# An attention and two-MoE kernel on one core: a third buffer for queries and keys, and another order of the first loads

## The chip, the cores and the metric

The kernel runs on one core of a Trainium2 chip. A core has TensorE (PE, matmuls; PEld is its weight load), VectorE (DVE), ScalarE (ACT) and GpSimd (POOL), an SP queue that issues the DMAs, on-chip memory (SBUF) and eight matmul result banks (PSUM). The metric is the device time in microseconds of one execution; lower is better. Before the change three runs gave 1020.78, 1024.65 and 1021.84 us, so the median is 1021.84 us.

## The reference

The input has 4 batches, 8 heads, 576 positions, head size 64. Cut to what matters:

```python
cum    = cumsum(maximum(s, 0), axis=-1)            # one row of running sums per head
scores = q @ k.T / sqrt(64) - (cum[:, None] - cum[None, :])   # the second part at most 0
attn   = softmax(where(causal, -1e9, scores))
x      = (attn @ v) as 2304 x 512
x      = ((x @ w_a) * (x @ w_b)) @ w_out           # 512 -> 1536 -> 512
out    = maximum(x @ w_in2, 0)**2 @ w_out2         # 512 -> 2048 -> 512
```

The weights of the MoE parts come as 64-bit floats; the kernel decodes their words on the chip.

## The kernel before

The work of all engines is recorded as operations, and a planner (`Plan.order`, a list scheduler with cost guesses per operation) fixes the order in which each engine issues them. Every engine then works its own list in order, so an instruction that waits holds all that stand behind it on its engine. The planner knows a rank per stream ("first" before "att", "moe", "late", "fill"), the buffers of each tag, and a `lag` by which an operation may be held back. Where it sees TensorE idle it puts filler matmuls (tile `glow`, weights and data `warm`) in the gap, which keep TensorE's clock up, and where a gap is longer than 400 ns it gives the next operation some more (`idle`).

Attention is done head by head. For batches 0 and 1 (`WHOLE = 2`) the query and the key of one head are loaded into the tiles `fq` and `fk` as 64 rows, a 65th row holds ones or the running sums, and one matmul in 32-bit floats (two records in the trace) gives a block of scores in a bank `st`. VectorE takes each block's maximum (`neg`), ScalarE the exponentials (`e`), TensorE transposes them (`pt`), either engine copies them (`ph`), TensorE multiplies with the values (`av`), and `u` is divided by the sums and stored to `xd`. For batches 2 and 3 two heads are loaded at a time (`raw`), scaled and split into high and low parts in tiles `T` (T1), `t2q`, `t2k`; each block is then two shorter matmuls. There the maximum is an instruction that also masks; the order calls it ISA, the profile CUSTOM_DVE.

The buffers that matter: two query tiles `fq` (tag T2q), used by head number modulo 2, and two `fk` (tag T2k); `t2q` and `t2k` of batches 2 and 3 take the same tags. The `raw` tiles have two buffers of their own, which the first sums also use (`ssb`, `spos`, `ch`, `cl`). So head 2 can load its query only when head 0's score blocks are done.

While the first batches' attention runs, the weights w_a, w_b and w_out are loaded (512 KB each, into room tiles `roomxh`, `roomxl`, `words`) and decoded on VectorE, ScalarE and GpSimd (`words`, `decode`). The first MoE matmuls (`ab`, `py`) start between attention work. Later chunks of x are read back from `xd` into `xl` and split (`xh`), and the words of w_in2 are decoded as well (`w2ir`, `w2it`). After about 400 us there is only matmul work with little else around it.

At the start the program issues fillers, and before the first score block of heads 0 and 2 it has six more:

```python
if b == 0 and i == 0 and hh in (0, 2):
    pl.ops[-1].idle = 6
```

Of the kernel before, what the change touches and what calls it, by code (L numbers as in the profile page):

```python
# [7 lines left out]
F32 = mybir.dt.float32  # L8
F32R = mybir.dt.float32r
# [254 lines left out]
def attention_moe_moe(tc, q, k, v, s, w_a, w_b, w_out, w_in2, w_out2, out):  # L264
# [61 lines left out]
    def at(shape, dtype, tag, bufs, name):  # L326
        return gated("at", shape, dtype, tag, bufs, name)
# [8 lines left out]
    def pe(cost, calls, out, ins, lag=0.0):  # L336
        pl.add({"PE": (cost, calls, False)}, [out], ins, lag=lag)
# [71 lines left out]
    kb = [(0, HEAD)] + [(HEAD + BODY * i, BODY) for i in range((S - HEAD) // BODY)]  # L409
    LAST = len(kb) - 1  # L410

    def load_values(b, p):

        t = at([P, NJ, P], F32, "val", 2, f"val{b}_{p}")
        j = 0
        while j < len(kb):
            k0, m = kb[j]
            j1 = j + 1
            while j1 < len(kb) and kb[j1][1] == m:
                j1 += 1  # L420
            dma(
                t[:m, j:j1].part(j),
                v[b, p, k0 : k0 + m * (j1 - j)].rearrange("(j t) c -> t j c", t=m), m * (j1 - j) * 0.5,
            )
            for i in range(j, j1):
                values[b, p, i] = t[:m, i].part(j)
            j = j1
# [2 lines left out]


    WHOLE = 2
    first_q = [at([P, S], F32, "T2q", 2, f"fq{i}") for i in range(2)]
    first_k = {}

    def load_first(b, hh):
        tq = first_q[hh % 2]
        tk = first_k[b, hh] = at([P, S], F32, "T2k", 2, f"fk{b}_{hh}")
        dma(tk[:D].part("x"), k[b, hh], S * 0.25)
        dma(tq[:D].part("x"), q[b, hh], S * 0.25)  # L440

# [3 lines left out]
    glow = mm_bank("glow")  # L445
    pl.stream = "fill"
    for i in range(FILL):
        pe(310, [("matmul", (glow, warm[:, :P], warm), {"start": True, "stop": True})], glow, [warm])
    pl.stream = "first"

    ssb = at([P, S], F32, "raw", 2, "ssb")[: B * H]
    dma(ssb, s.rearrange("b h s -> (b h) s"), 74)
    for hh in range(2):
        load_first(0, hh)

    ident = const([P, P], F32, "ident")
# [15 lines left out]
    plain = at_const([P, P], BF16, "plain")  # L472
    act("copy", P, plain, ident)

    spos = at([P, S], F32, "raw", 2, "spos")[: B * H]
    dve("tensor_scalar_max", S, spos, ssb, 0.0)
    cum = at([P, S], F32, "kh", 1, "cum")[: B * H]
    dve("tensor_tensor_scan", S, cum, spos, spos, 0.0, ALU.add, ALU.bypass)
    for t in first_q:
        gps("memset", S, t[D : D + 1].part("c"), 1.0)  # L480
    ch, cl = (at([P, S], F32R, "raw", 2, z)[: B * H] for z in ("ch", "cl"))
    act("copy", S, ch, cum)
    dve("tensor_tensor", S, out=cl, in0=cum, in1=ch.bitcast(F32), op=ALU.subtract, two=True)
    dma(cd[:, 0, :].part(0), ch.bitcast(F32), 74)
# [18 lines left out]
    RUNS = {(0, 1), (336, 0), (336, 2)}  # L503

    def load_pair(b, p, src, nm):
        t = at([P, S], F32, "raw", 2, f"raw{nm}")
        dma(t, src[b, 2 * p : 2 * p + 2].rearrange("h d s -> (h d) s"), 288)
        return t

# [23 lines left out]
    def prep_first(b, p):  # L533

        load_values(b, p)
        heads = []
        for hh in (2 * p, 2 * p + 1):
            if (b, hh) not in first_k:
                load_first(b, hh)
            tk = first_k[b, hh]  # L540
            dma(tk[D : D + 1].part("c"), cum[b * H + hh : b * H + hh + 1], 2)
            tq = first_q[hh % 2]
            scaled(S, tq[:D].part("x"))
            heads.append((tq, tk))
        return heads

    def prep(b, p):

        nm = f"{b}_{p}"
        tq = load_pair(b, p, q, f"{nm}q")  # L550
        tk = load_pair(b, p, k, f"{nm}k")
        load_values(b, p)
        scaled(S, tq)
        heads = []
        for h in range(2):
            hh = b * H + 2 * p + h
            t1 = operands()
            t2q = at([P, S], F32R, "T2q", 2, f"t2q{nm}_{h}")
            t2k = at([P, S], F32R, "T2k", 2, f"t2k{nm}_{h}")
            dma(t1[64:66, 1].bitcast(F32).part("ck"), cd[hh], 5)  # L560
            up, dn = slice(0, 64), slice(64, 128)
            xq, xk = t1[up, 0].part("xq"), t1[up, 1].part("xk")
            if h == 0:
                copy(S, xk, tk[up])
                copy(S, xq, tq[up])
                dma(t2q[up].bitcast(F32).part(0), xq.bitcast(F32), 144)
                subtract(S, t2q[dn].part(1), tq[up], xq.bitcast(F32))
                subtract(S, t2k[up].part(0), tk[up], xk.bitcast(F32))
                dma(t2k[dn].bitcast(F32).part(1), xk.bitcast(F32), 144)
            else:  # L570
                hi = t2q[dn].part(1)
                copy(S, hi, tq[dn])
                dma(xq.bitcast(F32), hi.bitcast(F32), 144)
                subtract(S, t2q[up].part(0), tq[dn], hi.bitcast(F32))
                hi = at([P, S], F32, "kh", 1, f"kh{nm}")[dn]
                copy(S, hi.bitcast(F32R), tk[dn])
                dma(xk.bitcast(F32), hi, 144)
                dma(t2k[up].bitcast(F32).part(0), hi, 144)
                subtract(S, t2k[dn].part(1), tk[dn], hi)
            heads.append((t1, t2q, t2k))  # L580
        return heads
# [4 lines left out]
    def softmax(b, p, h, head, one):  # L586
# [11 lines left out]
        for i, pieces in enumerate(banks):  # L598
            ps = mm_bank(f"st{nm}_{i}") if b == 0 and i % 4 > 1 else bank(f"st{nm}_{i}")
            off = 0  # L600
            calls, cost, got = [], 0, []
            for blk, k0, kn in pieces:
                at_, m = kb[blk]
                qc = slice(at_, at_ + m)
                to = ps[:m, off : off + kn]
                diag = at_ >= k0 and at_ + m <= k0 + kn
                ks = slice(k0, k0 + kn)
                if b < WHOLE:
                    tq, tk = head
                    both = ((tq[: D + 1, qc], tk[: D + 1, ks]),)  # L610
                    cost += 4 * kn / 2.4 + 13
                else:
                    t1, t2q, t2k = head
                    both = ((t1[:66, 0, qc], t1[:66, 1, ks]), (t2q[:, qc], t2k[:, ks]))
                    cost += 2 * (kn / 2.4 + 15)
                calls += [("matmul", (to, *ab), {"stop": True}) for ab in both]
                if diag and b < MASKED:
                    tri = mask[:m, EDGE : EDGE + m]
                    calls.append(("matmul", (to[:, kn - m :], plain[:m, :m], tri), {"stop": True}))
                    cost += 70  # L620
                e, eo = place[blk]
                got.append((blk, k0, m, to, kn, diag, e[:m, eo + k0 : eo + k0 + kn]))
                off += kn
            if b < WHOLE:
                ins = [tq.part("x"), tq.part("c"), tk.part("x"), tk.part("c")]
            else:
                ins = [t1, t2q, t2k]
            if b < MASKED:
                ins += [plain, mask]

            for z, (_, _, kw) in enumerate(calls):
                kw.update(start=z == 0, skip_group_check=z > 0)
            pe(cost, calls, ps, ins)
            if b == 0 and i == 0 and hh in (0, 2):
                pl.ops[-1].idle = 6
            for blk, k0, m, to, kn, diag, _ in got:
                c = blk if k0 == 0 else nq
                if not diag or b < MASKED:
                    dve("tensor_reduce", kn, out=neg[:m, c : c + 1].part(c), in_=to, op=ALU.max, axis=AX.X, negate=True)
                    continue  # L640
                edge = EDGE + m
                dve(
                    "tensor_tensor_reduce", kn + 135, out=to, in0=to, in1=mask[:m, edge - kn : edge], op0=ALU.add,
                    op1=ALU.min, scale=-1.0, scalar=3.0e38, accum_out=neg[:m, c : c + 1].part(c),
                )
            held += got
            whole = [x for x in held if x[0] != LAST or pieces[0][0] == LAST]
            held = [x for x in held if x not in whole]
            if pieces[0][0] == LAST:
                dve(  # L650
                    "tensor_reduce", 2, out=neg[:, nq + 1 : nq + 2].part(nq + 1), in_=neg[:, nq - 1 : nq + 1],
                    op=ALU.min, axis=AX.X, reads=[neg.part(nq - 1), neg.part(nq)],
                )
            for blk, k0, m, to, kn, diag, ee in whole:
                c = blk if k0 == 0 else nq
                n_ = nq + 1 if blk == LAST else blk
                act(
                    "activation", kn + 360, ee.part((blk, k0)), to, AF.Exp, bias=neg[:m, n_ : n_ + 1].part(n_), scale=-1.0 if diag and b >= MASKED else 1.0,
                    accum_out=tot[:m, blk, int(c == nq) : int(c == nq) + 1].part(c), psum=True,
                )  # L660
# [939 lines left out]
```

## Time and profile before

| | |
|---|---|
| median of three runs | 1021.84 us |
| profiled execution, its time | 1023.91 us |
| its span, first to last instruction | 1022.1 us |
| TensorE busy | 1002.8 us (98%) |
| VectorE, ScalarE, GpSimd busy | 735.5, 603.9, 322.3 us |
| DMA | 240.58 MB, mean 235 GB/s |

The trace shows when each instruction began, how long it took and what ended the idle time before it. A matmul's end is modelled, so a busy TensorE may still lose time between matmuls.

### The profile page before, as it was taken

To read this page: it belongs to the slowest core of one execution; us is meant where nothing else is said; L and a number is where in the kernel's file an instruction comes from. 1 tells how busy PE (TensorE), PEld (TensorE's weight loads), DVE (VectorE), ACT (ScalarE), POOL (GpSimd) and SP (SyncE) were. 2 spreads that over 40 slices of the span, in tenths; PEclk is the share of its full clock that TensorE was granted. 3 is DMA by queue.
4 is the path that set the end of the run, shared out by engine and by line. 5 is a ranking of instruction groups with operands and counts; after the bars stand their busy time and mean duration, and the time that the engine had idled before them with its cause. 6 is when DMAs were issued, how large, how long until landed. Compare 5 with 4: busy or idle time off the path is not lost.

```text
span 1022.1 us, 16764 instructions
## 1 busy us (share of the span) xinstructions
PE 1002.8 (98%) x5612; PEld 867.8 (85%) x5619; DVE 735.5 (72%) x1546; ACT 603.9 (59%) x1373; POOL 322.3 (32%) x293
## 2 busy tenths in 40 slices
PE   9999999999999999999999999999999999999997
PEld 5766777777777778788889999999999999999997
DVE  5878876756677765565697898688767755876566
ACT  6777886565777643343344544487565766657552
POOL 2243134325454622101122323323335212431123
PEclk9999999999999999999999999999999999999999
DMA  7458896558778667857666668499968876678664
GB/s 226 131 157 256 273 288 186 152 150 258 228 199 246 185 212 262 275 183 233 206 207 207 208 206 273 164 336 363 344 219 322 313 260 231 246 273 319 220 233 165
DMA packets 138006, 240.58 MB, mean 235 GB/s; under 512 B 21320, under 2 KB 91072, under 8 KB 137920
## 3 DMA queue, kind: packets, MB, share of 16 engines
q1 hardware_dynamic: 137920, 239.52, 71.1%
q8 instruction: 44, 0.72, 0.3%
q14 instruction: 42, 0.34, 0.1%
HBM read 181.42 MB, written 52.11 MB: 228 GB/s over the span
## 4 chain that ended last, share of the span: by engine, by line
PE 75%; DMA 5%; DVE 2%; SPq 1%; ACT 1%; issue 0%; DVEq 0%; ACTq 0%
PE ab L261 14%; PE pa L261 9%; PE py L261 8%; PE po_0t L261 6%; PE pw L261 5%; PE pc L261 5%; PE wa L261 4%; PE st L261 3%; PE av L261 3%; PE pt L261 3%; PE wc L261 2%; PE pb L261 2%; PE po_2b L261 2%; PE po_1b L261 2%; PE po_0b L261 2%; PE po_3b L261 2%
## 5 line engine op out<-in xcount | busy, mean ns | idle before, releaser
L261 ACT ACTIVATE e<-st,neg 120x336 f32<-120x336 f32 (+2 forms) x192 | 93.5, 492 | 28.5 <-DVE neg L261 26.6
L261 PE MATMUL py<-g,wh 128*128 128x512 f32 x288 | 92.0, 401 | 1.4 <-DVE y L261 1.2
L261 PE MATMUL ab<-xh,wh 128*128 128x512 f32 x192 | 77.4, 403 | 0.0
L261 PE MATMUL ab<-xh,lo 128*128 128x512 f32 x192 | 75.0, 391 | 0.0
L261 PE MATMUL ab<-xl,wh 128*128 128x512 f32 x192 | 75.0, 390 | 0.0
L261 PE MATMUL pt<-ident,e 120*120 120x120 f32 (+2 forms) x480 | 68.0, 268 | 0.8 <-DVE ph L261 0.4
L261 PEld LDWEIGHTS pt<-ident,e 120*120 120x120 f32 (+2 forms) x480 | 51.2, 133 | 20.2 <-issue 9.2
L261 DVE CUSTOM_DVE_ANT_0 st<-st,mask 96x96 f32<-96x96 f32 (+4 forms) x120 | 53.7, 453 | 20.0 <-PE st L261 18.2
L261 PE MATMUL ab<-x,wh 128*128 128x512 f32 x192 | 65.8, 424 | 0.8 <-ACT a L261 0.7
L261 PEld LDWEIGHTS py<-g,wh 128*128 128x128 f32 x288 | 53.3, 190 | 12.6 <-DVE y L261 1.6
L261 PE MATMUL av<-ph,val 120*64 120x240 f32 (+3 forms) x512 | 58.7, 360 | 0.0
L261 PE MATMUL st<-fk,fq 65*120 65x336 f32 (+2 forms) x192 | 56.3, 408 | 1.7 <-ACT e L261 1.7
L261 ACT COPY ph<-pt 120x360 f32<-120x360 f32 (+3 forms) x81 | 36.5, 459 | 35.9 <-PE pt L261 34.8
L261 PE MATMUL py<-g,loo 128*128 128x512 f32 x144 | 56.9, 395 | 0.0
L261 PEld LDWEIGHTS av<-ph,val 120*64 120x64 f32 (+1 forms) x512 | 31.1, 136 | 24.9 <-issue 12.4
L261 DVE COPY ph<-pt 120x360 f32<-120x360 f32 (+3 forms) x79 | 39.8, 514 | 16.2 <-PE pt L261 14.9
L261 DVE TENSOR_TENSOR ab<-ab,a 128x512 f32<-128x512 f32 x36 | 25.2, 701 | 33.3 <-PE ab L261 28.7
L261 PEld LDWEIGHTS ab<-xh,lo 128*128 128x128 f32 x192 | 36.0, 188 | 7.7
L261 ACT COPY a<-ab 128x512 f32<-128x512 f32 x36 | 21.1, 586 | 35.7 <-PE ab L261 35.6
L261 PEld LDWEIGHTS ab<-xh,wh 128*128 128x128 f32 x192 | 36.1, 188 | 6.4 <-issue 0.4
L261 PEld LDWEIGHTS ab<-x,wh 128*128 128x128 f32 x192 | 33.7, 189 | 9.2 <-ACT a L261 1.6
L261 PEld LDWEIGHTS ab<-xl,wh 128*128 128x128 f32 x192 | 36.2, 188 | 5.9
(692 smaller groups left out, 3098.4 us busy)
## 6 DMA issues: line engine op xcount, KB each, us to landing
w<-w2q SPq DMA_DIRECT2D x48, 896.0 KB, 6.7
lo<-wlab SPq DMA_DIRECT2D x36, 512.0 KB, 4.7
w2q<-w2ip SPq DMA_DIRECT2D x48, 256.0 KB, 4.2
w2s<-w2op SPq DMA_DIRECT2D x48, 256.0 KB, 4.6
loo<-wlo SPq DMA_DIRECT2D x24, 384.0 KB, 5.5
w2ir<-in_moe_w_in SPq DMA_DIRECT2D x16, 512.0 KB, 5.7
w2or<-in_moe_w_out SPq DMA_DIRECT2D x16, 512.0 KB, 4.3
ws_0t<-w2s SPq DMA_DIRECT2D x12, 512.0 KB
```

Of the source, the lines that this page charges most:

```text
L261: getattr(eng, method)(*map(real, args), **{k: real(a) for k, a in kw.items()})
```

## The change

Seven edits go together. (1) T2q and T2k get three buffers each; the first three heads are loaded at the start, and head h of batches 0 and 1 uses query tile h modulo 3. (2) The `raw` tiles lose their own buffers: raw queries take T2q, raw keys T2k. (3) `ssb` and `spos` live in the tag e2, `ch` and `cl` in u. (4) The planner holds the first values back by 6000 ns (`SOONER`). (5) The planner counts 400 ns, not 310, for a filler. (6) The six fillers before head 0's first block go. (7) A third row of ones is written.

```diff
+    SOONER = 6000.0
@@ load_values
+                lag=0.0 if b or p else SOONER,
@@
-    first_q = [at([P, S], F32, "T2q", 2, f"fq{i}") for i in range(2)]
+    first_q = [at([P, S], F32, "T2q", 3, f"fq{i}") for i in range(3)]
@@ load_first
-        tq = first_q[hh % 2]
-        tk = first_k[b, hh] = at([P, S], F32, "T2k", 2, f"fk{b}_{hh}")
+        tq = first_q[(b * H + hh) % 3]
+        tk = first_k[b, hh] = at([P, S], F32, "T2k", 3, f"fk{b}_{hh}")
@@
-        pe(310, [("matmul", (glow, warm[:, :P], warm), {"start": True, "stop": True})], glow, [warm])
+        pe(400, [("matmul", (glow, warm[:, :P], warm), {"start": True, "stop": True})], glow, [warm])
-    ssb = at([P, S], F32, "raw", 2, "ssb")[: B * H]
+    ssb = at([P, S], F32, "e2", 3, "ssb")[: B * H]
-    for hh in range(2):
+    for hh in range(3):
         load_first(0, hh)
@@
-    spos = at([P, S], F32, "raw", 2, "spos")[: B * H]
+    spos = at([P, S], F32, "e2", 3, "spos")[: B * H]
-    ch, cl = (at([P, S], F32R, "raw", 2, z)[: B * H] for z in ("ch", "cl"))
+    ch, cl = (at([P, S], F32R, "u", 2, z)[: B * H] for z in ("ch", "cl"))
@@ load_pair
-        t = at([P, S], F32, "raw", 2, f"raw{nm}")
+        t = at([P, S], F32, f"T2{nm[-1]}", 3, f"raw{nm}")
@@ prep
-            t2q = at([P, S], F32R, "T2q", 2, f"t2q{nm}_{h}")
-            t2k = at([P, S], F32R, "T2k", 2, f"t2k{nm}_{h}")
+            t2q = at([P, S], F32R, "T2q", 3, f"t2q{nm}_{h}")
+            t2k = at([P, S], F32R, "T2k", 3, f"t2k{nm}_{h}")
@@ softmax
-            if b == 0 and i == 0 and hh in (0, 2):
+            if b == 0 and i == 0 and hh == 2:
                 pl.ops[-1].idle = 6
```

Since the planner decides, instructions move on every engine, up to about 400 us. Two places are shown, on the SP queue and on VectorE.

The SP queue at the program's start, before; `fk`, `fq` are the heads' keys and queries, `val` the values, `cum` the running sums, `cd` their copies, `roomxh` the words of w_a:

```order
L261 DMA ssb<-in_s 32x576
L261 DMA fk_0_79<-in_k 64x576
L261 DMA fq_87<-in_q 64x576
L261 DMA fk_1_93<-in_k 64x576
L261 DMA fq_102<-in_q 64x576
L261 DMA val_0_110<-in_v 96x128
L261 DMA val_0_110<-in_v 120x4x128
L261 DMA val_1_120<-in_v 96x128
L261 DMA fk_0_79<-cum 1x16x36
```

The same place now:

```order
L261 DMA ssb<-in_s 32x576
L261 DMA fk_0_79<-in_k 64x576
L261 DMA fq_86<-in_q 64x576
L261 DMA fk_1_93<-in_k 64x576
L261 DMA fq_101<-in_q 64x576
L261 DMA fk_2_109<-in_k 64x576
L261 DMA fq_113<-in_q 64x576
L261 DMA roomxh<-in_moe_w_a 128x4x256
L261 DMA fk_0_79<-cum 1x16x36
```

The running sums are the ninth DMA in both; the three loads of values ahead of them have become head 2's key and query and the words of w_a, which stood fourteenth.

VectorE in the first pairs of batch 2, before; `st_1_0_2` and its `neg` are a score block and its maxima, `w2it` and `w2ir` words of w_in2, `y` sums of the first MoE part's output, `xl` the x read back:

```order
L261 SCALAR_TENSOR_TENSOR w2it_2762<-w2ir_0_2628,w2it_2762 128x512
L261 TENSOR_TENSOR y_0_0_0_1328<-py_3_0_0_2748,y_0_0_0_1328 128x512
L261 ISA st_1_0_2_2773,neg_153<-st_1_0_2_2773,mask 120x288
L261 ISA neg_153 120x1
L261 TENSOR_SCALAR w2ir_0_2628<-w2ir_0_2628 128x512
L261 CAST xh_2318<-xl_2250 128x512
L261 TENSOR_REDUCE neg_153<-neg_153 128x1
L261 TENSOR_TENSOR y_0_0_1_1368<-py_3_0_1_2779,y_0_0_1_1368 128x512
```

The same place now; `raw_2k` is the next pair's keys, `ab_11` and `g_11` the last block of the first MoE product, which TensorE's next `py` group reads:

```order
L261 CAST kh_2_2745<-raw_2k 64x576
L261 TENSOR_TENSOR ab_11_1_2612<-ab_11_1_2612,a_11_2642 128x512
L261 CAST xh_2353<-xl_2265 128x512
L261 ISA st_1_0_2_2756,neg_164<-st_1_0_2_2756,mask 120x288
L261 ISA neg_164 120x1
L261 TENSOR_TENSOR g_11_2771<-ab_11_1_2612,g_11_2771 128x512
L261 TENSOR_REDUCE neg_164<-neg_164 128x1
```

The cast of xl stood behind the block's reduction and now stands ahead of it, with a cast of raw_2k before both; the product g_11 and both sums y come behind them. On the SP queue the load of 512 KB `lo` before these loads moves behind xl, and the DMAs that spread the sums of the last pair of batch 1 (`wide`) move ahead of another such load.

## Rows read from the trace of the kernel before

**Rows 1.** The page: busy time of TensorE, and the chain that ended last.

```profile
PE 1002.8 (98%) x5612; PEld 867.8 (85%) x5619; DVE 735.5 (72%) x1546; ACT 603.9 (59%) x1373; POOL 322.3 (32%) x293
PE 75%; DMA 5%; DVE 2%; SPq 1%; ACT 1%; issue 0%; DVEq 0%; ACTq 0%
```

**Rows 2.** Stretches: busy us (instructions) of PE, PEld, DVE, ACT, POOL; clock; DMA share; GB/s.

```profile
0.00:10.00 10.00, 8.55 (x27) 3.43 (x28) 3.34 (x4) 3.98 (x6) 3.15 (x26) 1.00 0.52 143
10.00:20.00 10.00, 9.94 (x57) 6.71 (x58) 8.04 (x25) 7.03 (x26) 0.00 (x0) 1.00 1.02 326
100.00:120.00 20.00, 19.84 (x101) 14.62 (x101) 17.14 (x35) 17.13 (x36) 1.28 (x1) 1.00 0.81 266
232.00:234.00 2.00, 2.00 (x13) 1.71 (x12) 1.43 (x5) 1.36 (x7) 0.34 (x1) 1.00 0.98 223
234.00:236.00 2.00, 2.00 (x12) 1.64 (x11) 1.88 (x4) 0.59 (x3) 0.00 (x0) 1.00 1.05 360
242.00:244.00 2.00, 2.00 (x9) 1.63 (x8) 1.74 (x9) 1.73 (x6) 1.45 (x2) 0.65 0.37 108
244.00:246.00 2.00, 2.00 (x7) 1.62 (x7) 0.28 (x1) 1.29 (x4) 1.92 (x2) 0.50 0.49 134
```

**Rows 3.** Timeline of weight loads: start, us, what, count, idle before and its end.

```profile
6.55 0.15 PEld L261 LDWEIGHTS <-warm 128*128 128x128 bf16 x1 [0.28 <-issue]
6.97 1.45 PEld L261 LDWEIGHTS <-warm 128*128 128x128 bf16 x7 [0.28 <-issue]
8.54 1.18 PEld L256 LDWEIGHTS <-warm 128*128 128x128 bf16 x6
9.84 0.40 PEld L261 LDWEIGHTS st<-fk,fq 65*120 65x120 f32 x2
```

**Rows 4.** Timeline of the SP queue at the start.

```profile
3.70 1.57 SPq L261 DMA_DIRECT2D val<-in_v  x3
5.39 1.23 SPq L261 DMA_DIRECT2D fk<-cum  x2
```

**Rows 5.** DMA issues of 8.2 to 13 us: KB each, us to landing.

```profile
roomxh<-in_moe_w_a SPq DMA_DIRECT2D x1, 512.0 KB, 4.6
```

**Rows 6.** Instructions of tile fk: landing of its DMAs.

```profile
DMA to landing us min/median/max: 2.2/2.8/3.6
```

**Rows 7.** Timeline of VectorE, 17 to 23 us.

```profile
17.03 0.41 DVE L261 TENSOR_SCALAR roomxl<-roomxh 128x512 int32<-128x512 int32 x1
...
17.48 0.69 DVE L261 SCALAR_TENSOR_TENSOR roomxl<-roomxh,roomxl 128x512 int32<-128x512 int32 x1
...
19.48 0.44 DVE L261 TENSOR_SCALAR fq<-fq 64x576 f32<-64x576 f32 x1
...
22.44 0.67 DVE L261 TENSOR_REDUCE neg<-st 120x1 f32<-120x336 f32 x2 [1.38 <-PE st L261]
```

**Rows 8.** Timeline of ScalarE, 11 to 25 us.

```profile
11.98 0.54 ACT L261 ACTIVATE e<-st,neg 120x336 f32<-120x336 f32 x1 [5.16 <-DVE neg L261]
...
23.61 0.68 ACT L261 ACTIVATE fq<-fq 64x576 f32<-64x576 f32 x1
24.19 0.52 ACT L261 ACTIVATE e<-st,neg 120x336 f32<-120x336 f32 x1
```

**Rows 9.** Timeline of the SP queue, 220 to 234 us.

```profile
220.89 2.52 SPq L261 DMA_DIRECT2D wide<-rd  x4
...
229.38 0.33 SPq L261 DMA_DIRECT2D xd<-u  x1
...
232.02 0.53 SPq L261 DMA_DIRECT2D lo<-wlab  x1
...
233.61 0.38 SPq L261 DMA_DIRECT2D xl<-xd  x1
```

**Rows 10.** Timeline of all engines, 239 to 241 us.

```profile
239.60 0.43 DVE L261 CAST xh<-xl 128x512 fp32r<-128x512 f32 x1 [3.11 <-DMA xl<-xd]
...
240.77 0.47 PE L261 MATMUL st<-T 66*120 66x456 f32 x1 [2.08 <-ACT e L261]
```

More of the change, by code (lines that the diff above doesn't have):

```diff
@@ L541, in prep_first @@
             dma(tk[D : D + 1].part("c"), cum[b * H + hh : b * H + hh + 1], 2)
-            tq = first_q[hh % 2]
+            tq = first_q[(b * H + hh) % 3]
             scaled(S, tq[:D].part("x"))
```

## The prediction

> **What bounds the kernel now.** I read the page's busy times and its chain first. TensorE is busy 98% of the span and has 75% of the chain that ended last [rows 1]: a change of order helps only where TensorE stood still or did filler matmuls, and both programs have the same real matmuls in number and shape (that the order shows; only fillers differ, 67 before and 62 after). Second, I read busy time by stretch. In the first 10 us VectorE worked 3.34 us and ScalarE 3.98 us, and in the next ten 8.04 and 7.03 [rows 2]: the two engines that do the softmax stand idle while loads come in. From 100 to 120 us they work 17.1 us of 20 each, so there a head start on TensorE can be lost again to them. Third, the start and the places with a wait. The first real weight load stands at 9.84 us, behind 21 fillers and six more that are planned before the first score block; the fillers start 0.43 us apart until 6.97 us (512 columns, so 1.2 GHz) and 0.21 us apart after it (1.45/7; 2.4 GHz) [rows 3]. The largest stall later is at 238 us: VectorE waits 3.11 us for the load of x (xl), stands before a maximum that ScalarE needs, and TensorE waits 2.08 us until 240.77 [rows 10]. Then the granted clock drops to 0.65 and 0.50 in 242 to 246 us [rows 2]; against full speed that is 2 x 0.35 + 2 x 0.50 = 1.7 us. This place costs 3.8 us.
>
> **The change part by part.** All sums are made against the profiled execution: span 1022.1 us, time 1023.91 us, so 1.8 us lie around the span, and it is 2.07 us above the median 1021.84 us.
>
> *Start.* The six fillers before the first score block go (8.54 to 9.84 us: 1.30 us), and two of the 21 before them are planned later (0.42 us). TensorE's queue is free for the first block at 9.84 - 1.72 = 8.1 us. But the block also needs the row of running sums (fk<-cum). That DMA is the ninth in the SP queue before and after, so it is issued at about 5.4 us again [rows 4]; what stands ahead has changed. Before: 4 loads of heads (144 KB each, by their shape) and 336 KB of values. After: 6 loads of heads and the 512 KB of w_a, 464 KB more, since the values wait their 6 us lag. The DMAs of fk need 2.2 to 3.6 us to land [rows 6], and the w_a load needed 4.6 us [rows 5]. If the sums land as their quickest did, 5.4 + 2.2 = 7.6 us, the fillers decide and 1.7 us are won. If they land behind w_a, which is issued as the eighth at about 5.0 us and lands at 9.6, the first block comes at 9.7 us and 0.1 us is won. I take 0.5 us, nearer to the row of w_a.
> The Trainium skill, page "DMA: Bandwidth & Descriptors", section "Queues, rings and completion order", says that each DMA engine takes its descriptors in ring order, with one ring per issuing queue. It speaks against the change: small sums behind 512 KB of words. The trace agrees, with 2.2 KB taking 2.2 us or more to land; by the rule alone the term is 0.1 us, without it 1.7.
>
> *Words before the softmax.* w_a is now the eighth load in the SP queue, not the fourteenth, and its decoding stands among head 0's maxima: on VectorE one shift (0.41 us) and one combine (0.69 us) [rows 7], on ScalarE one scaling ahead of the first exponential, in its idle 5.16 us [rows 8], and one between head 0's exponentials. Head 0 can come out 1.1 us later by this, but the work had to be done anyway and stood in head 1's chain before. So the price is between -1.1 us and nothing, and it is part of the next term.
>
> *The third head early.* Before, head 2 shares head 0's query buffer: it is scaled on VectorE at 19.48 us, and its first block reaches VectorE at 22.44 us after an idle 1.38 us; its first exponential is at 24.19 us, behind the scaling of head 3's query (0.68 us) [rows 7, 8]. After, head 2's operands are loaded at the start and scaled before the first exponential, so its blocks can follow head 1's at once. The idle 1.38 us can go whole, and 0.68 us of ScalarE moves into idle time: 2.06 us at most. What is late next: head 3's scaling now stands on VectorE ahead of head 1's last maximum, and its load still waits for head 0's blocks; if it lands as head 2's did (by 19.48 us), most of the 1.38 us turns into this wait. Bounds -1.1 to 2.06 us; I take half of 1.38, 0.7 us. The third buffer also frees the SP queue earlier for later heads; no long wait of TensorE on queries shows, so that counts nothing. The lost prefetch of the first raw pair of batch 2 counts nothing either: the order has its first cast at the same place on ScalarE, and the pool gives it the buffer of the last head but two, so the load lies beside two heads' work.
>
> *The load of x at 238 us.* Before, the chain is: rows of sums spread (wide<-rd, 220.89 us), xd stored at 229.38, the 512 KB lo load issued at 232.02, xl at 233.61, used at 239.60 [rows 9, 10]. After, wide is issued ahead of another 512 KB lo load and a copy (0.8 us of issues), and the lo load of 232 us moves behind xl: 0.6 us of issue and 512 KB at 223 to 360 GB/s [rows 2], 1.5 to 2.3 us. With the lead of 1.2 us from above, xl can land 1.2 + 0.8 + 0.6 + 1.9 = 4.5 us earlier, at 235.1. Against it: on VectorE the casts of raw_2k and xl now stand before the reduction of a score block and before the product that TensorE's first y group needs; before, a second y group (nine matmuls of 512 columns at 2.4 GHz, 1.9 us) filled the time. From xl's landing to TensorE's next step I count 0.43 us for the cast (its row) [rows 10], and some 1.3 us for reduction and product (two instructions of about the 0.69 us kind [rows 7]): 1.7 us. So TensorE goes on at 236.8 us in the best case and, if xl is no earlier, at 241.3 with 1.9 us less done, which is 2.4 us worse than before. Ends: 3.8 gained, 2.4 lost; with xl halfway at 237.4 it goes on at 239.1, and 1.7 us earlier with 1.9 us less done is no gain. As the transpose that starts the chain (rs of the last pair) also moves up in TensorE's order, I go a little to the early side: 1.0 us gained.
>
> *Fillers.* Net of the six at the start, one more filler stands elsewhere: 0.2 us at most, not counted. From 400 us the two orders differ little and nothing is expected there.
>
> Sum: 0.5 + 0.7 + 1.0 = 2.2 us off the profiled 1023.91 us gives 1021.7; brought to the median, 1021.84 - 2.2 = 1019.6 us.
>
> **Rivals.**
> 1. *The stall at 238 us goes whole, and the clock stays up.* For it: 512 KB less ahead of xl, and everything before it comes sooner. Against: the casts stand earlier on VectorE. With 1.0 at the start, 1.4 from head 2 and 3.8 here, 6.2 us: 1015.6 us.
> 2. *The lead is eaten.* VectorE and ScalarE are 86% busy from 100 to 120 us [rows 2], decoding words that TensorE needs; a lead of TensorE ends in a wait for them, and head 3's query replaces head 2's as the late one, so the third buffer does not do what it says. At 238 us gain and loss balance. Only some 0.2 us is left: 1021.6 us.
> 3. *Slower: VectorE is held by raw_2k and xl.* If the two loads land as late as before (239.6 us), the casts hold up reduction and product: 2.4 us lost, and the lead is gone as well, since the load sets the pace: 1024.2 us; more if the longer idle time brings a longer half clock. It decides from where xl lands later than about 237.4 us. For it: the DMA share is 0.98 to 1.05 there [rows 2]. Against: the lo load is out of its way.
>
> **How the numbers follow.** The forecast has 0.47 (its own spread is 1017 to 1022 us), rival 1 0.23, rival 2 0.18, rival 3 0.12. About 0.5% (5.1 us) is what a measurement of this kernel can tell from no change: faster is below 1016.7 us, slower above 1026.9. Faster: nearly all of rival 1 and a little of the forecast's own spread, 0.26. Slower: the tail of rival 3 and what I have not seen in a reordered program, 0.09. Same: 0.65. The range goes from 1.1 us below rival 1 to 0.8 us above rival 3, 1014.5 to 1025.0 us; a tenth is left out on each side, or a little less.
>
> **What would show it.** Start: the first score block's weight load between 8.1 and 9.8 us (9.3 expected), and fk<-cum landing behind w_a. Head 2: its first maximum near 21.2 us instead of 22.44, with VectorE's idle time before it now in front of head 3's scaling. The stall: VectorE's wait for xl or raw_2k near 236 us, its length, and whether the granted clock falls after it. Wrong would be: a first block later than 10 us; a lead at head 2 that is gone by 130 us; a new stall of more than 3 us; or a clock drop in another place.

## The result and the profile after

The changed kernel took 1033.07 us (median of 14 runs, 1023.77 to 1037.45), the kernel before 1020.12 us (14 runs beside it, 1016.45 to 1024.65). The ratio is 1.0108, 95% interval 1.0082 to 1.0133: slower by about 13 us, where 1019.6 us was forecast and 1025.0 us was the upper end. One thing is needed to read the numbers: in 3 of the 14 runs the granted clock stayed at full until the end, and these took 1023.77 to 1025.23 us; in the other 11 the mean granted clock was 0.989 to 0.996, and they took 1030.66 to 1037.45 us. The run profiled first (1024.52 us, span 1022.7) is one of the three. So its page shows only a part of the loss, and a second profile of the same kernel (e1, 1042.4 us, longer than all 14) shows where the clock went.

The page after, beside [rows 1]: busy times and the chain. Nothing in it tells that the kernel became slower.

```profile
PE 1001.8 (98%) x5614; PEld 866.1 (85%) x5614; DVE 734.5 (72%) x1552; ACT 599.7 (59%) x1361; POOL 333.4 (33%) x300
PE 86%; DMA 4%; DVE 3%; issue 2%; ACT 2%; POOL 1%; SPq 1%; DVEq 0%; POOLq 0%; ACTq 0%
```

The stretches of [rows 2], after, in the run whose clock stayed up (columns as there: the five engines, then clock, DMA share, GB/s):

```profile
0.00:10.00 10.00, 7.03 (x21) 2.76 (x22) 3.29 (x4) 5.32 (x8) 3.92 (x27) 1.00 0.62 172
10.00:20.00 10.00, 10.00 (x58) 6.83 (x57) 7.77 (x23) 7.16 (x25) 2.94 (x3) 1.00 0.95 302
242.00:244.00 2.00, 2.00 (x12) 1.68 (x11) 1.97 (x4) 0.00 (x0) 0.53 (x1) 1.00 0.85 112
244.00:246.00 2.00, 2.00 (x12) 1.71 (x11) 1.97 (x8) 1.51 (x5) 1.63 (x1) 1.00 0.93 318
```

In the first 10 us TensorE worked 7.03 us where it had worked 8.55. The half clock after 242 us is gone. At the start, the weight loads that answer to [rows 3] and the SP queue that answers to [rows 4]:

```profile
6.04 1.39 PEld L261 LDWEIGHTS <-warm 128*128 128x128 bf16 x7 [0.19 <-issue]
9.41 0.28 PEld L261 LDWEIGHTS st<-fk,fq 65*120 65x120 f32 x2 [1.98 <-issue]
```

```profile
4.99 0.59 SPq L261 DMA_DIRECT2D roomxh<-in_moe_w_a  x1
5.70 1.22 SPq L261 DMA_DIRECT2D fk<-cum  x2
```

The 512 KB of w_a are issued first and the sums' rows behind them. The first score matmul waits for these rows, and here is the difference between the two profiles of the same program. After, and then e1 (start, duration, and in brackets the idle time of the engine before it and what ended it):

```profile
9.45 0.80 PE L261 MATMUL st<-fk,fq 65*120 65x336 f32 x2 [1.52 <-DMA fk<-cum]
```

```profile
10.44 0.80 PE L261 MATMUL st<-fk,fq 65*120 65x336 f32 x2 [2.31 <-DMA fk<-cum]
```

In e1 the rows land a microsecond later, TensorE stands still for 2.31 us instead of 1.52, and some 3 us after it resumed the granted clock goes to half (1.2 GHz of 2.4). The stretches of e1 show it in the sixth number:

```profile
0.00:12.00 12.00, 8.23 (x29) 3.68 (x30) 3.69 (x5) 5.33 (x8) 3.93 (x27) 1.00 0.67 183
12.00:20.00 8.00, 8.00 (x27) 5.14 (x26) 5.02 (x15) 4.57 (x17) 1.28 (x1) 0.57 0.96 309
20.00:28.00 8.00, 7.78 (x27) 4.28 (x27) 4.36 (x11) 3.29 (x10) 2.72 (x2) 0.57 0.61 193
28.00:40.00 12.00, 12.00 (x87) 8.03 (x86) 9.87 (x29) 7.82 (x24) 1.28 (x1) 1.00 0.18 55
```

TensorE is busy for 15.78 of the 16 us and starts 54 matmuls in them, against 87 in the 12 us behind. The trace's clock records put the half clock at 13.17 to 26.82 us, 13.65 us.

That is half of e1's half clock. The records hold 13.65 us more: 6.83 us from 258.93, 3.41 from 689.00 and 3.41 from 719.73. Each of these begins within a microsecond of the end of another wait:

```profile
258.74 0.60 PE L261 MATMUL st<-T 66*120 66x456 f32 x1 [1.84 <-ACT e L261]
688.04 0.62 PE L261 MATMUL pa<-b11h,w 128*128 128x384 f32 x2 [1.55 <-DMA w<-w2q]
719.44 1.11 PE L261 MATMUL po_0t<-g_0t,ws_0t 128*128 128x384 f32 x3 [2.64 <-DMA ws_0t<-w2s]
```

A second loss stands late, also in the run with full clock. TensorE's waits from 500 to 760 us (what waited, for what: us in all, times, the longest), before and then after:

```profile
PE py L261 <- DVE y L261: 1.2, 1, 1.2
PE pw L261 <- DVE gl L261: 0.7, 1, 0.7
```

```profile
PE po_0t L261 <- DMA ws_0t<-w2s: 2.6, 2, 2.2
PE py L261 <- DVE y L261: 1.5, 1, 1.5
PE wa L261 <- ACT s1w L261: 0.8, 2, 0.6
```

Two places fix the size of it: the one stalled `py` group near 517 us, and the last of the 72 matmuls of `po_0t` with `g_1t`, the same work in both. Before:

```profile
519.42 0.72 PE L261 MATMUL py<-g,wh 128*128 128x512 f32 x2 [1.24 <-DVE y L261]
L261 PE MATMUL po_0t<-g_1t,ws_0t x72: 334/334/336, 698.5 to 943.4; 128*128 128x384 f32 x72
```

After:

```profile
517.52 0.74 PE L261 MATMUL py<-g,wh 128*128 128x512 f32 x2 [1.54 <-DVE y L261]
L261 PE MATMUL po_0t<-g_1t,ws_0t x72: 334/334/338, 699.1 to 944.3; 128*128 128x384 f32 x72
```

Before it takes 943.4 - 519.42 = 424.0 us from the one to the other, after 944.3 - 517.52 = 426.8: 2.8 us lost where the prediction expected nothing.

### The profile page after: what moved, and what is told of

It is laid out like the page before. It is cut to its first block, busy times and chain, and to the rows that moved or that the text cites. A ratio compares the mean times of both kernels' runs of the same rounds, so it can differ in the third digit from the quotient of the medians.

```text
span 1022.7 us, 16712 instructions
## 1 busy us (share of the span) xinstructions
PE 1001.8 (98%) x5614; PEld 866.1 (85%) x5614; DVE 734.5 (72%) x1552; ACT 599.7 (59%) x1361; POOL 333.4 (33%) x300
## 4 chain that ended last, share of the span: by engine, by line
PE 86%; DMA 4%; DVE 3%; issue 2%; ACT 2%; POOL 1%; SPq 1%; DVEq 0%; POOLq 0%; ACTq 0%
PE ab L261 17%; PE pa L261 9%; PE py L261 7%; PE st L261 6%; PE po_0t L261 6%; PE pc L261 5%; PE pw L261 5%; PE av L261 5%; PE wa L261 4%; PE pt L261 4%; PE pb L261 2%; PE wc L261 2%; PE po_0b L261 2%; PE po_2b L261 2%; PE po_1b L261 2%
## 5 line engine op out<-in xcount | busy, mean ns | idle before, releaser
L261 ACT ACTIVATE e<-st,neg 120x216 f32<-120x216 f32 (+2 forms) x192 | 93.3, 490 | 30.0 <-DVE neg L261 26.2
L261 POOL TENSOR_TENSOR wl<-roomxl,wh 128x512 fp32r<-128x512 f32 x20 | 26.7, 1346 | 51.4 <-ACT wh L261 46.1
```

The source lines that it names most:

```text
L261: getattr(eng, method)(*map(real, args), **{k: real(a) for k, a in kw.items()})
```

## The experiments

Fourteen kernels ran, the first the changed kernel itself. "Wait" is TensorE's idle time before the first score matmul, "half clock" how long the granted clock was at half in the first 40 us of the profiled run; the median and the ratio are over all runs of that kernel (4 to 12), and the ratio does not follow the medians exactly.

| | wait, us | half clock, us | median, us | ratio to before, interval |
|---|---|---|---|---|
| e1 after again | 2.31 | 13.65 | 1033.21 | 1.0134 [1.0084, 1.0185] |
| e2 six fillers back | 1.76 | 17.07 | 1031.91 | 1.0103 [1.0068, 1.0138] |
| e3 before, no six | 0 | 0 | 1018.28 | 0.9984 [0.9965, 1.0003] |
| e4 cover | 0 | 0 | 1024.93 | 1.0063 [1.0038, 1.0088] |
| e5 before, words ahead, no six | 2.65 | 13.65 | 1025.91 | 1.0049 [1.0027, 1.0071] |
| e6 after, words behind | 0 | 6.83, from 22 us | 1030.65 | 1.0090 [1.0056, 1.0123] |
| e7 before, words ahead, six kept | 0 | 0 | 1023.90 | 1.0035 [1.0009, 1.0062] |
| e8 after, no lag | 1.94 | 27.31 | 1038.61 | 1.0177 [1.0145, 1.0209] |
| e9 after, 310 ns | 1.61 | 6.83 | 1021.94 | 1.0023 [1.0002, 1.0044] |
| e10 after, 310 ns, cover | 0 | 0 | 1021.09 | 1.0011 [0.9996, 1.0025] |
| e11 buffers only | 0 | 0 | 1030.47 | 1.0100 [1.0078, 1.0122] |
| e12 e4 with a late load moved | 0 | 0 | 1027.55 | 1.0068 [1.0043, 1.0094] |
| e13 310 ns, six, sums ahead | 0 | 0 | 1020.91 | 1.0009 [0.9992, 1.0026] |
| e14 before, a late load moved | 0 | 0 | 1020.47 | 1.0011 [0.9990, 1.0033] |

**e1: the changed kernel unaltered.**

> The changed kernel again, unaltered, for a profile of its longer executions (11 of 14 were 1030 to 1037 us at a mean granted clock of 0.989 to 0.996; 3 were 1024 to 1025 at 1.000). Clock theory: TensorE idles 1.7 us before the first score block because the six fillers are gone, and in most executions the granted clock then falls to half in the first 30 us and stays there for 10 to 20 us; the profile shows half clock there, about 1033 us. Order theory: the half clock lies at a later stall of the new order (63, 130 or 167 us).

The loss came back, and the longest stretch of half clock stands at the start (rows above).

**e2: the six fillers back.**

```diff
-            if b == 0 and i == 0 and hh == 2:
+            if b == 0 and i == 0 and hh in (0, 2):
```

> The changed kernel with the six fillers before head 0's first score block again; nothing else moves, and the first block waits for its loads until after them anyway. Clock theory: every execution at a mean clock of 0.998 or more, 1017 to 1022 us. Order theory: no change, 1030 to 1036 us in most executions, since the stall that lowers the clock is still there.

Six fillers do not reach to the rows' landing: TensorE still waits 1.76 us and the clock is halved for 17.07 us. Their removal alone is not the cause: with them back, 25 fillers stand ahead of the first block and the ratio is 1.0103.

**e3: the kernel before without its six fillers.**

```diff
-            if b == 0 and i == 0 and hh in (0, 2):
+            if b == 0 and i == 0 and hh == 2:
```

> The kernel before without its six fillers ahead of head 0's first score block; nothing else moves. Clock theory: the first block comes up to 1.3 us sooner, but the executions become slow as those of the change, 1027 to 1034 us at a mean clock under 0.997. Order theory: 1019 to 1020 us, some 1 us faster than before.

The first block comes at 8.09 us and nothing is lost. In the order of before the rows land in time even without the six.

**e4: the changed kernel with 14 fillers there.**

```diff
-            if b == 0 and i == 0 and hh == 2:
-                pl.ops[-1].idle = 6
+            if b == 0 and i == 0 and hh in (0, 2):
+                pl.ops[-1].idle = 6 if hh else 14
```

> The changed kernel with 14 fillers (3.0 us at full clock) before head 0's first score block, so that TensorE works until about 10.8 us whatever lands; nothing else moves. Gap theory (the idle 1.9 to 2.7 us while the sums' row lands lets the clock fall to half at 11 to 13 us for 14 to 17 us): the clock holds, 1023 to 1026 us, first block at 10.8 us. Rival (what follows the first block in the new order is too thin for the clock): half clock as in the two runs before, 1030 to 1037 us.

The rows still land behind w_a, but TensorE works until then:

```profile
10.07 0.73 PE L261 MATMUL st<-fk,fq 65*120 65x336 f32 x2
```

The block starts later than in the first profile of after (10.07 against 9.45 us), and yet the kernel is 8 us faster than the changed one (1024.93 against 1033.07; 4.6 us by the ratios): what cost the time is TensorE standing still, not the late block. The 1024.93 us agree with the three runs of the changed kernel that kept their clock. What is left, 1.0063, I put down to the second loss: up to the stalled `py` group e4 is level with e3 (515.23 and 514.67 us).

**e5: the kernel before without the six, and w_a's load moved ahead of the sums' rows.** One DMA moves in the SP queue, nothing else.

```diff
+        i, j = seq.index(self.words0), seq.index(self.sums[0])
+        seq.insert(j, seq.pop(i))
```

> The kernel before without the six fillers (1018.3 us) with one DMA moved: the first load of w_a is issued ahead of the sums' rows, not behind them; the rest keeps its order. Gap theory: the first block waits until about 10 to 10.5 us, TensorE idles about 2 us, the clock falls in most executions: 1025 to 1029 us. Rival: the clock holds, the first block is later but the time stays 1018 to 1020 us.

```profile
10.71 0.80 PE L266 MATMUL st<-fk,fq 65*120 65x336 f32 x2 [2.65 <-DMA fk<-cum]
```

Against e3 (1018.28 us) this one DMA costs 7.6 us, or 6.6 by the ratios; of its 12 runs the two with full clock took 1019 and 1020 us. So one load ahead of the rows is enough to bring the first loss into the old order.

**e6: the changed kernel with w_a's load moved behind the sums' rows** (the same edit the other way round).

> The changed kernel with one DMA moved: the load of w_a is issued behind the sums' rows of heads 0 and 1; the rest keeps its order. Gap theory: the sums land by 8.8 us, TensorE idles under 1.2 us, the clock holds in most executions: 1023 to 1025 us. Rival: 1030 to 1036 us as the change.

The first wait is gone, and some 15 us later the clock is halved around the next one: from 22.36 us, while TensorE still waits, for 6.83 us. VectorE and TensorE there:

```profile
21.21 0.56 DVE L266 TENSOR_SCALAR fq<-fq 64x576 f32<-64x576 f32 x1 [2.38 <-DMA fq<-in_q]
```

```profile
22.77 1.46 PE L266 MATMUL pt<-ident,e 120*120 120x120 f32 x6 [1.58 <-DVE ph L266]
```

It is head 3's query: with three heads loaded at the start the fourth is the late one, and it stands behind the words in the queue.

**e7: the kernel before with its six fillers, and w_a's load ahead.**

```diff
+        i, j = seq.index(self.words0), seq.index(self.sums[0])
+        seq.insert(j, seq.pop(i))
```

> The kernel before, its six fillers kept, with the load of w_a ahead of the sums' rows. Gap theory: the fillers last until 9.8 us, the idle time is under 0.8 us, the clock holds in most executions: 1020 to 1022 us. Rival: the same 1020 us; with the run that leaves the six out this tells the wait from the idle time.

Here 27 fillers hide the late rows in the profiled run (first block at 9.78 us, clock full, span 1016.9). Over 12 runs it is still 3.6 us slower than before, with mean clocks from 0.991 to 1.000: the likely reason is that the cover has no margin. Only one of the 12 was profiled, but both ends move between traces: after and e1 have the same order and their first blocks, which wait for the rows, stand at 9.45 and 10.44 us, and the same 21 fillers end at 8.92 us in the kernel before and at 8.58 us here.

**e8: the changed kernel without the lag.**

```diff
-    SOONER = 6000.0
+    SOONER = 0.0
```

> The changed kernel without its lag: SOONER is 0, so head 0's first values stand ahead of the sums' rows again and w_a behind them; three buffers, three heads at the start, 400 ns per filler and no six fillers stay. Theory (the lag alone brings both losses: words ahead of the sums, and the late loads ws_0t behind the stores): no idle time of TensorE over 1 us before 30 us, granted clock at full until 200 us, no wait for ws_0t near 692 us, 1017 to 1021 us, a ratio of 0.997 to 1.001. Rival A (the third buffer or the third head's loads are what harms): sums' rows still land later than 9 us, half clock in the first 30 us, 1026 us or more. Rival B (the loss at 80 to 140 us stays lost without the stall at 238 us to make up for it): clock full, 1023 to 1025 us.

My theory fell here. w_a stands behind the rows again, and the kernel is the slowest of all. Its chain from 5 to 13 us:

```profile
6.21 3.05 DMA fk<-cum
9.26 0.14 issue
9.40 3.61 PE st L261 x15
```

Head 2's two loads and two loads of values are ahead of the rows, which land at 9.26 us. The fillers end at 7.5 us, TensorE waits 1.94 us, and the clock is halved for 27.31 us. So in the new order the rows land late without w_a ahead of them, too: 240 KB more stand ahead of them than in the kernel before, and they are issued at 6.21 us instead of 5.39. The lag alone is not the cause.

**e9: the changed kernel with 310 ns per filler.**

```diff
-        pe(400, [("matmul", (glow, warm[:, :P], warm), {"start": True, "stop": True})], glow, [warm])
+        pe(310, [("matmul", (glow, warm[:, :P], warm), {"start": True, "stop": True})], glow, [warm])
```

> The changed kernel with 310 ns per filler for the planner, as before: w_a still ahead of the sums' rows and no six fillers, but the planner then puts three loads of ws_0t ahead of the next stores to w2s, as in the kernel before. Theory (two losses apart, the clock at the start and some 4 us late): half clock for 13 to 17 us in the first 30 us, no wait for ws_0t near 692 us, 1027 to 1030 us. Rival (the wait for ws_0t is covered, and the start alone makes the loss): no better than the changed kernel, 1031 to 1035 us.

Faster than expected. With 310 ns the planner puts 24 fillers ahead of the first block, not 19, and the order late is that of before (no wait for ws_0t). There is still a wait of 1.61 us, but the half clock was 6.83 us at the start (3.41 us more from 687.94, behind a wait of 1.87 us), and 7 of its 12 runs kept a mean clock of 0.998 or more. The edit that I had counted at nothing carries most of the loss: 11 us of 13 by the medians, 8.7 of 11.0 by the ratios. The number of fillers ahead of the block does not explain it: e2 had 25 there and the same order of the first loads, waited 1.76 us and kept its loss. What keeps the clock up in more of e9's runs stays open.

**e10: the same, with 14 fillers before head 0.**

```diff
-        pe(400, [("matmul", (glow, warm[:, :P], warm), {"start": True, "stop": True})], glow, [warm])
+        pe(310, [("matmul", (glow, warm[:, :P], warm), {"start": True, "stop": True})], glow, [warm])
-            if b == 0 and i == 0 and hh == 2:
-                pl.ops[-1].idle = 6
+            if b == 0 and i == 0 and hh in (0, 2):
+                pl.ops[-1].idle = 6 if hh else 14
```

> The changed kernel with 310 ns per filler for the planner and 14 fillers before head 0's first block: w_a still ahead of the sums' rows, but TensorE has work until they land, and the loads of ws_0t stand ahead of the stores. Theory (both losses taken away, the rest of the change costs and brings nothing): clock full in the first 200 us, no wait for ws_0t, 1017 to 1021 us. Rival (the loss at 80 to 140 us counts): clock full, 1023 to 1026 us.

With cover at the start and the old order late, everything else in the change is worth nothing that can be measured: 1.0011 [0.9996, 1.0025]. That holds although its first block comes as late as 11.74 us (10.05 in the profile of before).

**e11: the buffers alone** (no lag, 310 ns, six fillers kept).

```diff
-    SOONER = 6000.0
+    SOONER = 0.0
-        pe(400, [("matmul", (glow, warm[:, :P], warm), {"start": True, "stop": True})], glow, [warm])
+        pe(310, [("matmul", (glow, warm[:, :P], warm), {"start": True, "stop": True})], glow, [warm])
-            if b == 0 and i == 0 and hh == 2:
+            if b == 0 and i == 0 and hh in (0, 2):
```

> The kernel before with the buffers alone: three each for queries and keys, three heads at the start, raw words and first sums in other homes; no lag, 310 ns per filler, the six fillers before head 0. Theory (the third buffer's lead is lost to VectorE and ScalarE by 140 us, and the start is covered): clock full, 1018 to 1022 us, a ratio of 0.998 to 1.002. Rival (the lead of head 2 lasts): 1015 to 1018 us. Rival (the third head's loads delay the sums past the fillers): a gap over 1 us before the first block, half clock, 1026 us.

All three expectations missed: clock full at the start, and 10 us slower. At 135 us TensorE runs out of work, as the planner foresaw, and after 20 fillers it waits on top:

```profile
135.29 4.49 PE L256 MATMUL py<-warm 128*128 128x512 bf16 x20
...
143.60 0.64 PE L261 MATMUL st<-fk,fq 65*120 65x456 f32 x1 [1.74 <-ACT e L261]
```

The clock is then at half for 3.4 us (145.44 to 148.85 us). TensorE came here ahead of its words: while it stands, GpSimd, VectorE and ScalarE still decode (`roomxl`, `roomxh`, `words` lead the list of waits in this stretch); that this is the cause is argued from these lists, not tested. These places give about 4.5 + 1.7 + 1.7 = 8 us, of 10.

What e11 does show is the worth of the lag. e10 and e13 have the same three buffers, 310 ns and a covered start, and both have the lag: they run at 1.0011 and 1.0009, have 2 and 4 fillers between 128 and 150 us where e11 has 25, and no wait over 1 us there. Each differs from e11 in one more thing (the number of fillers at the start; the place of w_a's load), but at the start e11 had no wait and the clock at full anyway. So the lag is most likely what keeps the third buffer from costing 10 us; e8, the other kernel without it, is the slowest of all.

**e12: e4 with the second late load ws_0t ahead of four stores.**

```diff
+        j = [n for n, o in enumerate(seq) if o in self.late0][1]
+        i = [n for n, o in enumerate(seq[:j]) if o in self.stores][-4]
+        seq.insert(i, seq.pop(j))
```

> The changed kernel with 14 fillers before head 0's first block (as in e4, which took 1024.9 us) and one load more moved: the second late load ws_0t (near 692 us) is issued ahead of the four stores to w2s behind which the planner put it. Theory (the late wait is that load behind the stores, and it is on the path): no wait of TensorE for ws_0t over 1 us, 2 us less than e4, 1022 to 1023.5 us. Rival (the wait only moves to the next thing that is late, or the stores are now late): as e4, 1024.5 to 1026 us.

The theory of the stores fell. The load is issued at 701.60 us, and TensorE's last matmul of po_0b there ends at 699.19 + 2.38 = 701.57:

```profile
701.60 0.32 SPq L268 DMA_DIRECT2D ws_0t<-w2s  x1
```

```profile
699.19 2.38 PE L268 MATMUL po_0b<-g_0b,ws_0b 128*128 128x384 f32 x12
702.61 0.79 PE L268 MATMUL po_0t<-g_0t,ws_0t 128*128 128x384 f32 x3 [1.04 <-DMA ws_0t<-w2s]
705.70 0.62 PE L268 MATMUL po_0t<-g_0t,ws_0t 128*128 128x384 f32 x2 [0.73 <-DMA ws_0t<-w2s]
```

What the load waits for is its buffer, which po_0b frees: the SP queue's own waits there have po_0b as what ended them (3.0 us in all in e12, 3.2 in the changed kernel). In the changed kernel it is the same:

```profile
698.06 0.35 SPq L261 DMA_DIRECT2D ws_0t<-w2s  x1
```

```profile
695.78 2.24 PE L261 MATMUL po_0b<-g_0b,ws_0b 128*128 128x384 f32 x12
703.00 0.80 PE L261 MATMUL po_0t<-g_0t,ws_0t 128*128 128x384 f32 x3 [2.17 <-DMA ws_0t<-w2s]
```

po_0b ends at 698.02, the load is issued at 698.06. TensorE's new order does po_0b right ahead of po_0t, so a load is issued when its reader is next. The medians of e12 and e4 (1027.55 and 1024.93 us, intervals overlapping) give no gain either.

**e13: three buffers, lag, 310 ns and six fillers, with w_a's load behind the rows.**

```diff
+        i, j = seq.index(self.words0), seq.index(self.sums[1])
+        seq.insert(j, seq.pop(i))
```

> The three buffers, three heads and the lag with 310 ns per filler and the six fillers before head 0, and w_a's words issued behind the sums' rows. Theory (with sums that land before the fillers end, no late load and no half clock, the three buffers are worth what is left): first block by 9.9 us, clock full, 1016.5 to 1019.5 us, at best 0.3% faster than before. Rival (head 3's query, which waits for head 0's buffer and stands behind the other words, holds VectorE as in e6): TensorE idle over 1 us near 21 us, half clock behind it, 1022 us or more.

First block at 9.24 us, clock full, and no gain. Head 3's query again holds VectorE for 2.51 us near 21 us; TensorE loses 0.78 us by it and keeps its clock.

**e14: the kernel before with its third late load ws_0t behind two stores.**

```diff
+        i = [n for n, o in enumerate(seq) if o in self.late0][2]
+        j = [n for n, o in enumerate(seq) if n > i and o in self.stores][1]
+        seq.insert(j, seq.pop(i))
```

> The kernel before with one DMA moved: the third late load ws_0t (issued at 695.3 us in the profile of before) goes behind the next two stores to w2s (as the planner orders it in the changed kernel). Theory (a load of ws_0t behind stores makes TensorE wait, and that wait is lost): a wait for ws_0t of 1.5 to 2.5 us near 702 us, a ratio of 1.001 to 1.003. Rival (there is slack for it): no wait, ratio 0.999 to 1.001.

No wait for ws_0t, and no loss by the runs: the order of before has slack there. That agrees with e12: the place in the SP queue is not what decides. Its profile does have a wait of 2.17 us for another load (`w<-w2q`, until 681.47 us), with the clock at half for 3.41 us; that stands ahead of the moved load, and e9 and e13 have the same wait without the move (1.87 and 1.82 us).

## Why the prediction was wrong

*Start: the step that failed.* "If they land behind w_a, which is issued as the eighth at about 5.0 us and lands at 9.6, the first block comes at 9.7 us and 0.1 us is won." The landing is right: w_a issued at 4.99, rows behind it, first weight load at 9.41 where 9.3 was expected. The price is wrong, since it left out that TensorE would stand still and what the clock does then. I subtracted times of the first block and so took the fillers as time to be won. They were TensorE's cover until the rows land, and without them the same microseconds are idle time, after which the granted clock is halved in most runs. Shown by e4 (the block even later, but no idle time: 8 us back) and e5 (one load moved: 7.6 us lost). The term is not +0.5 but, by the medians, about -8.5 us: 1033.07 less the 1024.5 of the runs that kept their clock. Not all of that need stand at the start: in e2's profile all of the half clock does (17.07 us), in e1's a half of it; but with the start covered (e4) 9 of 10 runs had a mean clock of 0.999 or more. The row that should have warned stood in [rows 2]: at 242 to 246 us a stall of 2.08 us had halved the clock for 3.4 us, and I priced it there and not here. The prediction did name "a clock drop in another place" among the signs of being wrong, but without a price.

The sentence on rings from the Trainium skill ("DMA: Bandwidth & Descriptors", "Queues, rings and completion order") pointed to the right cause: each DMA engine takes the descriptors of one ring in order, and so 2.2 KB of sums wait behind what was issued ahead of them. The runs agree: with one load moved ahead of them (e5 against e3) the first block goes from 8.09 to 10.71 us, and the rows of e1 took 4.02 us to land, by its chain. [rows 6], which had 3.6 at most, holds the loads of the keys as well as these rows, so it was no measure of the rows by themselves.

*Fillers: failed too.* "Net of the six at the start, one more filler stands elsewhere: 0.2 us at most, not counted." The 400 ns make the planner think that 19 fillers reach as far as 24 do, and they also shift the whole order to the end. e9 undoes that edit alone and gains 11 us. Of these the order gives about 5 us, by the runs that kept their clock (1019.25 us, median of five, against 1024.52); the rest is clock.

*Third head early: mechanism right, gain nil.* Head 2 no longer waits: its first maximum stands at 21.27 us, where 21.2 was expected and 22.44 was before. Head 3's scaling has taken over the wait, as I had put under rival 2. In after, VectorE at 19 to 21 us:

```profile
19.15 0.79 DVE L261 TENSOR_SCALAR fq<-fq 64x576 f32<-64x576 f32 x1 [0.92 <-DMA fq<-in_q]
...
21.27 0.65 DVE L261 TENSOR_REDUCE neg<-st 120x1 f32<-120x336 f32 x2
```

The half of 1.38 us that I took is not seen in any total: e10 and e13 are level with before. e11 shows where a lead of TensorE ends without the lag: in fillers and, as far as its lists tell, a wait for the engines that decode.

*The load of x at 238 us: right in the trace, wrong as a gain.* xl is issued at 231.84 instead of 233.61 us, its cast at 235.73 waits for nothing, and the clock stays up. But the stall that I let it repay was that of one execution. e3, e7 and e14 have the same order there, and the same matmul of theirs waits 0.26, 0.36 and 0.26 us, where [rows 10] has 2.08. In e7:

```profile
237.69 0.47 PE L266 MATMUL st<-T 66*120 66x456 f32 x1 [0.36 <-ACT e L266]
```

The profiled execution of before took 1023.91 us, 3.8 us above the median of 14 runs, which is what I had worked out for this place (3.8 us). So in the median there was next to nothing to win.

*"From 400 us the two orders differ little and nothing is expected there": wrong.* From the `py` group at 517 us to the end of po_0t the changed kernel loses 2.8 us, and e4, by the same two places (515.23 and 943.8), 428.6 - 424.0 = 4.6 us. The wait for ws_0t is 2.6 us of it in both. It goes where the planner's 310 ns bring the old order back (e9, e10, e13; there TensorE waits 1.3 to 2.1 us for `w<-w2q` instead), and stays when a DMA is moved (e12). It can also bring a half clock of its own: 3.41 us in e1, from 719.73, and in e6, from 708.44 behind a wait of 1.86 us. That it costs time was seen only together with the whole late order; a kernel with that wait alone wasn't made.

The sum: 1020.1 + 4.4 (order, clock at full) + 8.5 (half clock in most runs, the greater part gone when the start is covered) = 1033 us. Of the rivals, 2 had the late query right, and 3, the slower one, had the wrong place: VectorE does not hold TensorE at 238 us.

Open is why a wait of 1.5 to 2.7 us leaves the clock up in one place or run and halves it in another: the first profile of after kept its clock through waits of 1.52 and 2.17 us (at 9.45 and 703.00), while others were followed by 3.4 to 27 us of half clock. None of the versions beats the kernel before by more than its interval; e3 comes nearest (0.9984 [0.9965, 1.0003]).

## What to carry to other kernels

A filler ahead of the first real work is not time to be won until the data's landing is shown to be earlier than the filler's end: price its removal as idle time of TensorE, with what the clock does after it, and not as a delay. Before counting on the repair of a stall, look whether the profiled execution is above the median by just that stall. Where a planner writes the order, a change of one of its costs is a change everywhere, and places far from the edit have to be read too.

## What the hardware did that I had not expected

Waits of TensorE of only 1.61 to 2.65 us before the first block (e1, e2, e5, e8, e9) were followed by a granted clock of one half for 6.83 to 27.31 us, beginning between 1.1 and 2.8 us after the work had resumed; in e6 it began during a wait of 1.58 us. It stayed at half although TensorE was busy nearly all the time (8.00 of 8.00 us in e1 from 12 to 20 us). In the first profile of after a wait of 1.52 us was followed by none. With a DMA of 512 KB issued just ahead of the 2.2 KB rows, the first block, which waits for the rows, stood at 9.45 to 10.71 us (after, e1, e2, e5, e9); in e3, which differs from e5 by that one load, it stood at 8.09 us and did not wait for them.
